# Linear attention with decay, then a GELU MLP, on one core: heads paired as h and h+4, reordered on chip, and an opening by single chunks

## Chip, core and metric

The kernel runs on one core of one Trainium2 chip. Its time is device time in microseconds (us). The core has a matmul engine (TensorE, "PE" in the profile, with its weight loads as "PEld"), a vector engine (VectorE, DVE), a scalar engine (ScalarE, ACT), GpSimd (POOL) and a queue engine (SyncE, SP). Matmul results go to PSUM, which has eight banks; 16 DMA engines move data, by transfers that POOL issues (loads that convert float32 to bf16) and SP issues (stores, and transposes of bf16 tiles within on-chip memory).

## The reference

Batch 4, 8 heads, sequence 768, head size 64; then an MLP with model width 512 and hidden width 2048, its rows being the 3072 tokens. Cut to what matters:

```python
def _attn_ref(q, k, v, lam):                      # q, k, v: (4, 8, 768, 64), lam: (8,)
    pos = np.arange(64); rel = pos[:, None] - pos[None, :]
    Dmask = np.where(rel >= 0, lam[:, None, None] ** rel[None], 0.0)
    lam_pow = lam[:, None, None] ** (pos[None, :, None] + 1)
    rev_pow = lam[:, None, None] ** (63 - pos[None, :, None])
    kv_state = zeros((B, H, D, D))
    for b in range(12):                           # blocks of 64 positions
        qb, kb, vb = ...
        intra = einsum('bhic,bhjc->bhij', qb, kb) * Dmask[None]
        intra = einsum('bhij,bhjd->bhid', intra, vb)
        inter = einsum('bhid,bhde->bhie', qb * lam_pow[None], kv_state)
        out[:, :, sl] = intra + inter
        kv_state = lam ** 64 * kv_state + einsum('bhsd,bhse->bhde', kb * rev_pow[None], vb)
    return out

h = x @ w_in                                      # x: (3072, 512), heads side by side
return 0.5 * h * (1 + erf(h / sqrt(2))) @ w_out   # exact GELU
```

## The kernel before

The sequence is cut into chunks of 128 positions: 6 per batch, 24 in all, chunk n being position block n // 4 of batch n % 4. Four chunks make a group (g = 0 to 5), which the MLP treats at once (512 tokens).

**Attention of a chunk.** q, k and v of all 8 heads are loaded by POOL as [128 positions, 8 heads, 64] (`load`, L66). k and q are transposed to [64 x 2 heads, 4 pairs, 128 positions]: a pair hp holds heads 2hp and 2hp+1, one in each half of the 128 partitions (HALVES). Chunks 0 to 7 are transposed by PE (`transposed`, L157) and copied out of PSUM by DVE or ACT; chunks 8 to 23 by a DMA that SP issues (`dma_transposes`, L173), straight from the loaded tile. Scores k q^T are 64-deep products per head (`scores` L179; from chunk 4 on in 64x64 quarters of the PE array, `scores_by_quarters` L190), masked by DVE (`masked` L199). Chunks from 4 on have a state per head (64x64), for two chunks in one tile: `from_states` (L222) multiplies it with qT, `from_values` (L231) adds masked scores times v. The output has the heads as the MLP's x wants them: head h in partition half h % 2 of column block h // 2. Since a state's half hi lies in row half hi and its output goes to column half hi, one product uses one of two diagonal quarters of the array; `turn` alternates the two chunks' banks, and eight dummy products (`apart`, L598 to 603) stand between the two turns where no scores do. The outputs leave PSUM by `empty_outputs` (L243) into xT, by ACT for chunks below 7, by DVE for chunk 7, and from chunk 8 on by DVE with the multiplication by lam_q (powers of lam along the position). For chunks 4 to 7 that multiplication is made in qT instead (`scaled`, L166). New states come from `next_products` (L203), `added` (L213) and `next_states` (L218). v times its decay, v_dec, is made by POOL (`decay_v`, L152).

**MLP.** First product and GELU in blocks (`mm1`, L421 and L424), second product for group 0 directly (`mm2`, L434), from group 1 on by seven half-size products instead of eight (`blocks_by_seven`, L277), for which DVE forms sums of GELU outputs (`g_sum`, L286) and of w_out (`w_out_sum`, L263).

**Order.** Each engine runs its own instructions in the order of the program. The opening (L495 to 541) is written out: attention of chunks 0, 1 and the transposes of 2, with dummy matmuls (`keep_warm`) in gaps; then the loop over MLP blocks (L672) puts attention work between blocks: group 0 by the table `group0` (L556; key i is ahead of block i, e = N1 is the first of the second product's 16 blocks), later groups by `todo`, a list of (place, function): place counts PE columns, B is one block of about 2048 columns, and "g + 10 * B" is ahead of block 10 of group g. A `visit` (L588) does the second half of attention for `done` chunks and scores for `asked` ones, on PE; `masks`, `empties`, `sums`, `new_states` are the DVE or ACT work behind it, placed separately. `begin_at` (L579) starts a chunk: DMA transposes on SP, v_dec on POOL. `prefetch` issues loads, 10 buffers for k and 8 each for q and v.

Group 0's plan of first-product blocks (kf is a column block of 128 of w_in):

```python
plan = [(kf, 1, two) for kf in range(6)] + [(0, 4, third), (4, 2, third)]
plan += [(kf, 1, three) for kf in range(6, 12)] + [(kf, 4, fourth) for kf in range(0, 12, 4)]
plan += [(kf, 1, slice(0, T)) for kf in range(12, NK2)]
```

Here `two` is chunks 0 and 1, `three` 0 to 2, `third` chunk 2, `fourth` chunk 3.

Of the kernel before, what the change touches and what calls it, by code (L numbers as in the profile page):

```python
# [15 lines left out]
def kernel(  # L16
# [14 lines left out]
    C = 128  # L31
# [82 lines left out]
    ln_col = consts.tile([128, HP], F32)  # L114
    lam_q = consts.tile([128, HP, C], F32)
# [9 lines left out]
    def make_powers():  # L125
        ln_r = ln.rearrange("p (hp hi) -> p hp hi", hi=2)
        for hi in range(2):
            p = slice(hi * D, (hi + 1) * D)
            nc.scalar.copy(ln_col[p, :, None], ln_r[p, :, hi:hi + 1])
        nc.scalar.activation(lam_m, ln, ACT.Exp, scale=negj)  # L130
        nc.scalar.activation(lam_c, ln_col, ACT.Exp, scale=float(C))
        for hp in range(HP):
            nc.scalar.activation(lam_q[:, hp, :], row, ACT.Exp, scale=ln_col[:, hp:hp + 1])
# [23 lines left out]
    def transposed(c, name, tag, empty):  # L157

        src, t_ps = getattr(c, name), bank([128, HP, C], BF16, tag, "t_ps")
        for hp in range(HP):  # L160
            nc.tensor.transpose(t_ps[:, hp, :], src[:, 2 * hp:2 * hp + 2, :], ident)
# [4 lines left out]
    def scaled(dst, src):  # L166
        nc.vector.tensor_mul(dst, src, lam_q)

    def transposes(c, tag="mh"):
        transposed(c, "k", tag, nc.scalar.copy)  # L170
        transposed(c, "q", "mh", scaled)

    def dma_transposes(c):  # L173
        c.kT = work_pool.tile([128, HP, C], BF16, tag="kT", name="kT", bufs=4)
        c.qT = work_pool.tile([128, HP, C], BF16, tag="qT", name="qT", bufs=6)
        nc.sync.dma_start_transpose(out=c.kT, in_=c.k.rearrange("p h d -> p (h d)"))
        nc.sync.dma_start_transpose(out=c.qT, in_=c.q.rearrange("p h d -> p (h d)"))
# [25 lines left out]
    def next_products(n, tag):  # L203

        kv_ps = bank([128, 2, HP, D], F32, tag, "kv_ps")
        for i, c in enumerate((live[n], live[n + 1])):
            for hp in range(HP):
                for hi, p in enumerate(HALVES):
                    nc.tensor.matmul(kv_ps[p, i, hp, :], c.k[:, 2 * hp + hi, :], c.v_dec[:, 2 * hp + hi, :],  # L209
# [12 lines left out]
    def from_states(chunks, o_ps, turn):  # L222

        for hp in range(HP):
            for hi, p in enumerate(HALVES):
                i = hi ^ turn
                c = chunks[i]
                nc.tensor.matmul(o_ps[i][p, hp, :], states[c.n - i][p, i, hp, :], c.qT[p, hp, :],  # L228
                                 start=(hp == 0), stop=False, skip_group_check=True)

    def from_values(c):  # L231
        v = c.v if c.early else c.v_dec
        for hp in range(HP):
            for hi, p in enumerate(HALVES):
                nc.tensor.matmul(c.o_ps[p, hp, :], v[:, 2 * hp + hi, :], c.sc_m[:, hp, hi, :],  # L235
# [478 lines left out]
```

## Time and profile before

| | us |
|---|---|
| median of 3 runs | 206.71 (205.24 to 207.11) |
| the profiled execution | 206.0 |
| its span | 204.2 |

| engine or line | busy us | instructions | mean ns |
|---|---|---|---|
| first product, 128x512 | 67.7 | 304 | 379 |
| GELU, ACT 128x512 | 52.6 | 88 | 597 |
| g_sum, DVE | 35.6 | 50 | 752 |
| masks without decay, DVE | 25.4 | 40 | 681 |
| v_dec, POOL | 24.8 | 23 | 1109 |
| x from o_ps with lam_q, DVE | 10.5 | 16 | 680 |
| state products, PE 64x64 | 8.0 | 160 | 219 |
| score products, PE 64x64 | 7.2 | 320 | 218 |
| x from o_ps, ACT | 4.0 | 7 | 586 |
| kT from t_ps, ACT | 2.4 | 4 | 588 |
| qT from t_ps, scaled, DVE | 2.8 | 4 | 688 |
| kT or qT from t_ps, plain, DVE | 3.4 | 8 | 421 |
| apart_ps, PE 64x64 | 1.5 | 32 | 216 |

A mean is the time of one instruction from start to end; PE's overlap, so that its slots are shorter. The profile's chain of waits, its last part in order of time, is followed back from the last instruction; it gives PE's slots.

### The profile page before, as it was taken

What the parts mean: (1) busy time and instruction counts of PE and PEld (TensorE: products, weight loads), DVE (VectorE), ACT (ScalarE), POOL (GpSimd) and SP (SyncE); (2) the same over time, 40 slices, a digit from 0 to 9 for tenths busy, and PEclk for the clock granted to TensorE, in tenths of its full rate; (3) what the DMA queues carried; (4) which work ended last, traced back from release to release, by engine and by line L of the source; (5) the groups of instructions that cost most, each with busy time, mean ns of one, the idle gap of its engine ahead of it and who ended that gap; (6) DMA issues with size and microseconds to landing.
All of it is one profiled execution on the core that took longest, in us unless ns stands there. A gap on an engine that the chain in (4) does not pass through costs nothing. (4 is left out here: it accounts for less than half of the span.)

```text
span 204.2 us, 4909 instructions
## 1 busy us (share of the span) xinstructions
PE 197.0 (96%) x2105; PEld 131.2 (64%) x2105; DVE 124.8 (61%) x202; ACT 80.7 (39%) x142; POOL 96.2 (47%) x112
## 2 busy tenths in 40 slices
PE   7889999999999999999999999999999999999992
PEld 2457574556874888646678646688645788445881
DVE  3743426773574699845999815968807857132482
ACT  4946653324565400273520273520264510477200
POOL 8999963899998922599998402000000000000000
PEclk9999999999999999999999999999999999999999
DMA  5999999999999999799999992200500000500014
GB/s 114 156 174 176 199 207 194 155 215 158 178 194 141 154 157 152 232 126 160 117 162 155 231 189 55 56 0 3 206 1 3 0 0 3 205 0 0 3 51 154
DMA packets 102373, 24.70 MB, mean 121 GB/s; under 512 B 92880, under 2 KB 99536, under 8 KB 102352
## 3 DMA queue, kind: packets, MB, share of 16 engines
q0 software_dynamic: 80688, 13.37, 89.4%
q1 hardware_dynamic: 21664, 11.02, 26.8%
q8 instruction: 16, 0.26, 0.5%
q14 instruction: 5, 0.04, 0.1%
HBM read 27.27 MB, written 6.29 MB: 164 GB/s over the span
## 5 line engine op out<-in xcount | busy, mean ns | idle before, releaser
L424 ACT ACTIVATE g_t<-h_ps 128x512 bf16<-128x512 f32 (+2 forms) x101 | 58.2, 576 | 82.0 <-PE h_ps L421 81.8
L421 PE MATMUL h_ps<-x_t,w_in_t 128*128 128x512 bf16 (+3 forms) x488 | 87.0, 334 | 0.4
L421 PEld LDWEIGHTS <-w_in_t 128*128 128x128 bf16 x488 | 44.1, 98 | 38.0 <-issue 1.3
L291 DVE TENSOR_TENSOR g_sum<-g_t 128x1024 bf16<-128x1024 bf16 x50 | 35.6, 752 | 12.6 <-ACT g_t L424 12.6
L317 PEld LDWEIGHTS <-g_sum 128*128 128x128 bf16 x400 | 38.6, 98 | 5.7 <-DVE g_sum L291 0.7
L155 POOL TENSOR_TENSOR v_dec<-v_t,lam_m 128x512 bf16<-128x512 bf16 x23 | 24.8, 1109 | 22.5 <-PE o_ps L235 10.2
L201 DVE TENSOR_TENSOR sc_m<-sc_ps,cmask 128x512 bf16<-128x512 f32 x40 | 25.4, 681 | 13.0 <-PE sc_ps L195 13.0
L68 POOL DMA_DIRECT2D k_t<-in_k_dram x24 | 22.3, 928 | 1.9 <-DMA w_out_t<-in_moe_w_out_dram 1.7
L68 POOL DMA_DIRECT2D v_t<-in_v_dram x24 | 21.7, 906 | 3.0 <-DMA w_out_t<-in_moe_w_out_dram 1.7
L68 POOL DMA_DIRECT2D q_t<-in_q_dram x24 | 21.8, 910 | 2.4 <-DMA w_out_t<-in_moe_w_out_dram 2.2
L317 PE MATMUL r_ps<-w_sum,g_sum 128*128 128x256 bf16 x160 | 19.1, 273 | 0.0
L317 PEld LDWEIGHTS <-g_t 128*128 128x128 bf16 x160 | 15.7, 98 | 2.9
L434 PE MATMUL o_ps<-w_out_t,g_t 128*128 128x512 bf16 x64 | 15.2, 379 | 0.0
L215 DVE TENSOR_TENSOR tmp<-kv_ps,state 128x512 f32<-128x512 f32 x8 | 5.1, 684 | 12.8 <-PE kv_ps L209 12.8
L251 DVE TENSOR_TENSOR x_t<-o_ps,lam_q 128x512 bf16<-128x512 f32 x16 | 10.5, 680 | 1.0 <-PE o_ps L235 1.0
L317 PE MATMUL p_ps<-w_out_t,g_sum 128*128 128x256 bf16 x80 | 9.7, 273 | 0.4 <-DVE g_sum L291 0.4
L434 PEld LDWEIGHTS <-g_t 128*128 128x128 bf16 x64 | 5.9, 98 | 6.2
L484 PE MATMUL idle_ps<-idle 128*128 128x256 bf16 (+1 forms) x33 | 8.6, 400 | 1.2 <-DVE idle L102 1.2
L317 PE MATMUL s_ps<-w_sum,g_sum 128*128 128x256 bf16 x80 | 9.6, 273 | 0.0
L317 PE MATMUL p_ps<-w_sum,g_t 128*128 128x256 bf16 x80 | 9.6, 273 | 0.0
L317 PE MATMUL q_ps<-w_sum,g_t 128*128 128x256 bf16 x80 | 9.6, 273 | 0.0
L317 PE MATMUL q_ps<-w_out_t,g_sum 128*128 128x256 bf16 x80 | 9.6, 273 | 0.0
(68 smaller groups left out, 153.4 us busy)
## 6 DMA issues: line engine op xcount, KB each, us to landing
out_dram<-o_sb SPq DMA_DIRECT2D x9, 512.0 KB, 2.8
k_t<-in_k_dram POOLq DMA_DIRECT2D x24, 128.0 KB, 6.9
q_t<-in_q_dram POOLq DMA_DIRECT2D x24, 128.0 KB, 7.4
v_t<-in_v_dram POOLq DMA_DIRECT2D x24, 128.0 KB, 7.3
w_out_t<-in_moe_w_out_dram POOLq DMA_DIRECT2D x4, 512.0 KB, 10.1
w_in_t<-in_moe_w_in_dram POOLq DMA_DIRECT2D x7, 256.0 KB, 7.3
out_dram<-o_sb SPq DMA_DIRECT2D x5, 256.0 KB, 6.0
wide_w<-in_moe_w_in_dram SPq DMA_DIRECT2D x1, 512.0 KB, 4.1
```

Of the source, the lines that this page charges most:

```text
L68: nc.gpsimd.dma_start(raw[n, name], chunk_of(name, n))
L155: eng.tensor_mul(c.v_dec, c.v, lam_m[:, :, None].to_broadcast((128, H, D)))
L201: nc.vector.tensor_mul(c.sc_m[:, :, hi, :], c.sc_ps[hi], mask)
L215: nc.vector.tensor_add(tmp, kv_ps, states[n])
L251: nc.vector.tensor_mul(c.x_o, c.o_ps, lam_q)
L291: nc.vector.tensor_tensor(gsum[i][:, ks, :], g_t[:, ka + k:ka + k + n4, ta], g_t[:, kb + k:kb + k + n4, tb], op=op)
L317: nc.tensor.matmul(o, left[i](k, slice(u * C, (u + 1) * C)), right[i](k), start=(begin and k == 0), stop=(k == KH - 1), skip_group_check=True)
L421: nc.tensor.matmul(h_ps[:, k, :], w_in_t[:, ki, (kf + k) * 128:(kf + k + 1) * 128], x_t[:, ki, cols], start=(k == 0 and ki == 0), stop=(ki ...
L424: nc.scalar.activation(g_t[:, kf:kf + ks, cols], h_ps, ACT.Gelu)
L434: nc.tensor.matmul(om[io], g_t[:, kf, io * C:(io + 1) * C], w_out_t[:, kf, :], start=(kf == 0), stop=(kf == NK2 - 1))
L484: nc.tensor.matmul(idle_ps[0][:, :cols], idle[:, :128], idle[:, :cols], start=True, stop=True)
```

## The change

Pairs are now heads h and h+4: partition half hi holds heads 4hi to 4hi+3. A state's row half is then the upper bit of the head, and its output's column half the lower bit, so that four state products in a row use four different quarters. To bring q and k into this order ahead of the transposes, a copy (`ordered`) makes k_p and q_p, two buffers each; chunks 0 to 3, which have no state to multiply, keep the old order. `apart` is gone. The scaling of chunks 4 to 7 by lam_q moves from qT to the emptying of o_ps (`emptied`), which is now by half of the heads for two chunks at once, and always on DVE.

```diff
     def make_powers():
         ln_r = ln.rearrange("p (hp hi) -> p hp hi", hi=2)
-        for hi in range(2):
-            p = slice(hi * D, (hi + 1) * D)
-            nc.scalar.copy(ln_col[p, :, None], ln_r[p, :, hi:hi + 1])
+        for hi, p in enumerate(HALVES):
+            nc.scalar.copy(ln_x[p, :, None], ln_r[p, :, hi:hi + 1])
+            nc.scalar.copy(ln_col[p], ln[p, hi * HP:(hi + 1) * HP])
...
     def transposes(c, tag="mh"):
         transposed(c, "k", tag, nc.scalar.copy)
-        transposed(c, "q", "mh", scaled)
-    def dma_transposes(c):
...
+        transposed(c, "q", "mh", nc.vector.tensor_copy)
+    def ordered(c, name, copy):
+        src = work_pool.tile([128, HP, 2, D], BF16, tag=name + "p", name=name + "_p", bufs=2)
+        copy(src, by_upper_bit(getattr(c, name)))
+        setattr(c, name + "_p", src)
+    def dma_transposed(c, name):
...
+        nc.sync.dma_start_transpose(out=dst, in_=src.rearrange("p s r d -> p (s r d)"))
...
-    def from_states(chunks, o_ps, turn):
-        for hp in range(HP):
-            for hi, p in enumerate(HALVES):
-                i = hi ^ turn
...
+    def from_states(chunks):
+        o_ps = [bank([128, 2, 2, C], F32, tag, "o_ps") for tag in ("o", "t")]
+        for i, c in enumerate(chunks):
+            for s in range(HP):
+                for hi, p in enumerate(HALVES):
+                    nc.tensor.matmul(o_ps[hi][HALVES[s % 2], s // 2, i, :], states[c.n - i][p, i, s, :], c.qT[p, s, :],
+                                     start=(i == 0 and s < 2), stop=False, skip_group_check=True)
...
+    def emptied(n, hi):
...
+        nc.vector.tensor_mul(xT[n // M][:, s, off:off + 2 * C].rearrange("p s (i t) -> p s i t", i=2), o_ps[hi],
+                             lam_q[:, s, None, :].to_broadcast((128, 2, 2, C)))
     def outputs(c):
...
+        empty = nc.vector.tensor_copy if c.n == 0 else nc.scalar.copy
...
-    N1 = 21
+    N1 = 19
...
+        plan = [(kf, 2, chunk) for chunk in (first, second) for kf in (0, 2)] + [(4, 2, two), (6, 2, two)]
+        plan += [(0, 4, third), (4, 4, third)]
+        plan += [(kf, 1, three) for kf in range(8, 12)] + [(kf, 4, fourth) for kf in range(0, 12, 4)]
...
+    nc.scalar.copy(w_in_t[:, :, :256], wide_w)
     make_powers()
...
-    nc.scalar.copy(w_in_t[:, :, :256], wide_w)
     keep_warm(2)
     scores(c)
-    keep_warm(9, new=False)
-    outputs(live[1])
-    c = early(2)
-    transposed(c, "k", "mh", copy)
-    transposed(c, "q", "mo", copy)
-    keep_warm(1)
+    early(2)
...
+        0: [lambda: keep_warm(2, new=False)],
+        1: [lambda: keep_warm(7), lambda: outputs(live[1])],
+        2: [lambda: k_transposed(2)],
+        3: [lambda: q_transposed(2)],
+        4: [lambda: scores(live[2]), lambda: keep_warm(7)],
+        5: [lambda: outputs(live[2])],
+        7: [lambda: k_transposed(3)],
+        8: [lambda: q_transposed(3), lambda: next_states(0, next_products(0, "t")), lambda: scores(live[3])],
+        10: [lambda: outputs(live[3])],
+        18: [lambda: next_states(2, next_products(2, "t"))],
+        e: [w_out_sums, lambda: both_ordered(4, copy), lambda: decay_v(live[4], nc.vector)],
         e + 8: [lambda: transposes(live[4])],
-        e + 9: [lambda: transposes(live[5], "o")],
+        e + 9: [lambda: both_ordered(5, nc.scalar.copy), lambda: transposes(live[5], "o")],
         e + 10: [lambda: visit([], [4, 5], "t o"), lambda: masks(5, 4)],
-        e + 11: [lambda: transposes(live[6])],
-        e + 13: [lambda: visit([4, 5], []), lambda: empties(4, 5)],
-        e + 14: [lambda: transposes(live[7])],
+        e + 11: [lambda: both_ordered(6, nc.scalar.copy), lambda: transposes(live[6])],
+        e + 13: [lambda: visit([4, 5], []), lambda: empties(4)],
+        e + 14: [lambda: both_ordered(7, nc.scalar.copy), lambda: transposes(live[7])],
...
+    def ordered_at(when, copy, *chunks):
+        for n in chunks:
+            for name in "kq":
+                at(when, lambda n=n, name=name: ordered(begun(n), name, copy))
+                at(when, lambda n=n, name=name: dma_transposed(live[n], name))
...
         if g == 1:
...
+            ordered_at(g - 0.07, nc.vector.tensor_copy, n)
+            ordered_at(g + 1 * B, nc.vector.tensor_copy, n + 1)
+            ordered_at(g + 6 * B, nc.vector.tensor_copy, n + 2)
+            ordered_at(g + 10 * B, nc.vector.tensor_copy, n + 3)
...
-            visit_at(g + 13 * B, [], [n, n + 1], (masks, n + 1, n))
+            visit_at(g + 14 * B, [], [n, n + 1], (masks, n + 1, n), banks="t o")
...
         for i, c_n in enumerate(later_on):
             begin_at(g + 0.57 + 0.03 * i, c_n)
+            if g == 1:
+                ordered_at(g + (19 + 2 * i) * B, nc.scalar.copy, c_n)
+            else:
+                ordered_at(g + (7 + i) * B, nc.vector.tensor_copy, c_n)
+            ordered_at(g + (27 + 2 * i) * B, nc.scalar.copy, c_n + 2)
```

`begin_at` now starts only v_dec; a chunk's copies and its DMA transposes have places of their own. In `visit`, the two calls of `from_states` with scores between them become one call ahead of everything else, and `from_values` takes both chunks at once.

More of the change, by code (lines that the diff above doesn't have):

```diff
@@ L254 @@
+        empty = nc.vector.tensor_copy if c.n == 0 else nc.scalar.copy
+        empty(xT[0][:, :, c.n * C:(c.n + 1) * C], o_ps)
     KH = NK2 // 2
@@ L298, in both @@
                 run()
[L299 to L305 removed]
+                if i in sums_at:
+                    g_sum((5, 2, 1, 6, 7)[sums_at.index(i)], 0)
+            return both
+        sums_at = range(10, 15)
+        blocks = [(with_sums(i, run), cost) for i, (run, cost) in enumerate(first)]
         left = {1: lambda k, t: gsum[1][:, k, t], 2: lambda k, t: gsum[2][:, k, t],
```

123 lines of the change are left out of this document (52 added, 71 removed).

## The prediction

> **What bounds the kernel now.** I read the page first: TensorE (PE) carries the span, and its granted clock never drops.
>
> ```profile
> span 204.2 us, 4909 instructions
> ...
> PE 197.0 (96%) x2105; PEld 131.2 (64%) x2105; DVE 124.8 (61%) x202; ACT 80.7 (39%) x142; POOL 96.2 (47%) x112
> ...
> PEclk9999999999999999999999999999999999999999
> ```
>
> The profiled execution took 206.0 us (1.8 around its span), 0.7 less than the median of the three timed runs, 206.7. The timeline of PE shows real work of the MLP beginning at 14.29 us and no gap worth naming afterwards but one of 0.41 us at 104.3 (p_ps waiting for DVE's g_sum). So a PE instruction that goes away after 14 us is worth its slot, unless something else then ends last. The chain of waits, read in order of time, prices the attention visits:
>
> ```profile
> 140.20 0.45 PE sc_ps L195 x28
> 140.65 0.22 PE o_ps L228 x8
> 140.87 0.57 PE o_ps L235 x16
> ...
> 169.34 0.34 PE o_ps L228 x8
> 169.68 0.22 PE apart_ps L602 x8
> 169.91 0.22 PE o_ps L228 x8
> 170.13 0.57 PE o_ps L235 x16
> ```
>
> Columns: start, length, what. Eight state matmuls (64x64 weights, 128 columns, two quarters of the array in turn) cost 0.22 us, 27 ns each; score matmuls of the same shape, which go round all four quarters, cost 0.45/28 = 16 ns each. Eight dummy apart_ps cost 0.22.
>
> The second limit shows in the first 55 us: the slices of the page have the DMA engines at 9 tenths there, and the timeline with each load's time to landing shows how close PE runs behind the data:
>
> ```profile
> 40.49 0.39 PE L161 MATMUL t_ps<-ident,k_t 128*128 128x128 bf16 x4
> ...
> 40.71 0.39 PE L161 MATMUL t_ps<-ident,q_t 128*128 128x128 bf16 x4
> ...
> 40.91 0.59 ACT L164 COPY kT<-t_ps 128x512 bf16<-128x512 bf16 x1 [0.46 <-PE t_ps L161]
> ```
>
> These are chunk 5's transposes. Its k was issued at 26.84 and landed 12.3 us later, at 39.1; its q at 28.36 and 11.6 later, at 40.0. PE has 0.7 us over q, no more.
>
> **The change, part by part.**
>
> *State matmuls.* Ten visits (two chunks each, 4 to 23) hold 16 of them, now 2 x 0.22. At the scores' rate they take 16 x 16 ns = 0.26; at an exact four at once, 0.22. Saving 0.18 to 0.22 per visit, 1.8 to 2.2 in all. *apart_ps:* four visits have it (32 instructions in the rows), 4 x 0.22 = 0.9 saved. Together 2.7 to 3.1; I take 2.9. The value matmuls keep number and shape.
>
> *Opening.* PE now does MLP blocks of chunk 0 alone while chunk 1's masks run, and of chunk 1 alone while chunk 2 loads. Chunk 0's x is ready when DVE has copied it, about 11.2 (outputs end at 10.4; DVE is at qT until 10.5, plus 0.69), if w_in's first 256 columns are cast by then: ACT does that right after the decay exponentials, 6.5 to 7.5; make_powers and the Gelu table move back by 1.05, the table is then in at about 10.8, before the first Gelu at 11.7. Following the landings (w_in 12.2, k2 13.1, q2 13.9, w_in 16.1 and 17.5), PE has finished the third chunk's block for kf 0 to 3 at 19.15 instead of 19.31, with eight columns of w_in (kf 0 to 7) done for chunks 0 and 1 instead of six; this surplus, two kf of 0.43 each, and the stalls of 0.2 to 0.3 that the new order fills bring the second half of group 0 (32.27 now) forward by 0.9 to 1.2. I take 1.05; k3, q3 (18.3, 20.0) and the last w_in (25.5) leave that room.
>
> *Where that goes.* Chunks 4 to 7 are now copied into the new order before PE transposes them. Chunk 4: DVE, behind the ten w_sum that end at 38.22 because they wait for w_out's landing; two copies, then PE, at 38.5 instead of 38.1. A DVE copy from SBUF to SBUF stands in no row: 0.42 (the copy from PSUM) above, about half of that below; I take 0.3. Chunk 5: ACT, two copies of 0.55 to 0.59 (the row of kT, same size), behind chunk 4's kT copy. q lands at 40.0, is copied by 40.6, PE transposes it at 40.65: 0.06 earlier than now. So of the 1.05 all but 0.06 is lost in front of chunk 5, and were there no gain in the opening, the ACT queue (39.86 + 3 x 0.48 + 0.11) would put q at 41.45, a loss of 0.75. Chunk 6 has 0.4 us over; chunk 7's q lands at 46.9, is ready at 47.5, and PE, 0.5 ahead by then, wants it at 47.55.
>
> *Emptying.* Chunks 4 to 7 no longer scale qT (4 x 0.27 of DVE saved), but ACT's three casts of x become scaled copies on DVE (0.68 each). x of chunks 6 and 7 is whole at about 54.8 and PE wants it at about 55.2: hidden, with 0.4 over.
>
> *Copies ahead of the DMA transposes, chunks 8 to 23.* Eight on DVE in group 1, eight more in groups 2 and 3 in a gap in which DVE idles 5.2 us, sixteen on ACT, which idles 12 us at the end of each group. By themselves they cost nothing; what matters is what they queue on. k_p and q_p have two buffers each, so chunk n+2's copy waits until chunk n's transpose has landed, 7 to 9 us after its issue at 53 to 60 us; and SP issues them one by one, 1.2 to 1.4 us each. Chunk 11: DVE's q copy waits for chunk 9's transpose (issued 54.1, landed about 62), is issued at 62.2 to 63.5, lands at 69.2 to 70.2; PE wants it at 70.4. DVE stands until 62.4 with five g_sums behind, which used to start at 58.5, but it has 5.1 us of idle time before 72. Zero, with 1.8 as the upper bound (landing 8.9 after 63.5).
> Chunk 17: its q copy sits on DVE in front of the `sums` of the visit at 92.8, and PE waits for these (they free the banks of its next products). q17 landed at 93.8, kv_ps was read at 94.33. Everything moves forward together, the load being released by PE's own kv_ps at 83.8, but the copy adds 0.3 and the later transposes of chunks 14 and 15 load the queue: 0 to 0.9, I take 0.2.
>
> Sum: 206.0 - 2.9 (visits) - 0.06 (opening less chunk 5's wait) + 0.2 (chunk 17) = 203.3; against the median of runs, 204.0. I give 203.6, between the two bases.
>
> **A rule that speaks against it.** Rows first: g_sum, 0.68 us as a rule, took 2.18 at 102.5 while POOL's v_dec ran (103.1 to 105.6), and two state products took 2.30 instead of 1.28 beside three v_dec. So DVE is held up by POOL on some operations, here with two SBUF operands; kT, qT and the masks, read from PSUM, are not. The Trainium skill (SBUF — State Buffer, "Who interferes with whom") makes it an exclusive lock, and puts a DVE copy from SBUF to SBUF in its fast two-port mode under it, against POOL's descriptor writing as well; no run here has such a copy yet. It is the third rival. For the price of such a copy, the Trainium skill (VectorE: DVE Perf Modes, "Mode 4×_2P — both tricks at once") would give an estimated 0.13 us of streaming for 512 bf16 elements, plus the fixed part; by it the sum would not change by 0.1.
>
> **The rivals.**
>
> 1. *The opening's gain survives* (chunk 5's q isn't what PE waits for, because loads land sooner or ACT copies faster than the rows say): up to 1.0 more, 202.3 to 203. Against it: landing times in that stretch are those of a full DMA queue, and the diff leaves the order of loads as it is. Chance 0.12.
>
> 2. *The two-buffer chain through DMA becomes the bound:* chunk 11 costs 1.8, chunk 17 0.9 instead of 0.2: 203.3 + 2.5 = 205.8 (206.2 as a median). For it: loads that land 8 to 11 us after their issue between 66 and 80 us; against it: loads of chunks 12 to 15 meet fewer transposes there than now. It decides from the point where a transpose takes over 7.5 us after 63. Chance 0.2.
>
> 3. *DVE's copies and POOL shut each other out.* POOL is busy nearly without break from 1.4 to 71 us. If each copy there stands behind a POOL instruction by the 1.5 us that g_sum did (2.18 - 0.68), then chunk 8's two copies push the masks of chunks 6 and 7 from 52.2 to about 54 with PE wanting them at 52.9 (1.0 lost), chunk 9's push x of chunks 6 and 7 past PE by 1.2, chunk 10's and 11's take DVE's reserve before the g_sums of m5, and chunk 17's costs 1.5: 3.7 at least, 206.8, slower than before (206.0); with rival 2's chunk 11, 208.6. It decides once the mean wait of a copy passes 1.2 us. Against it: POOL's rows of DMA issue show 0.88 to 0.95 whatever DVE does, so the hold may be a fraction of them. Chance 0.13.
>
> 4. *The quarters don't overlap:* state matmuls stay at 27 ns and only apart_ps goes: 206.0 - 0.9 - 0.06 + 0.2 = 205.2. Against it: scores show 16 ns with the same shapes, banks and order of quarters. Chance 0.05.
>
> **How the numbers follow.** My forecast, 203.6, has 0.5; its own range is 202.9 to 204.5 (the bounds of visits, of chunk 17, and the two bases). The range for 8 in 10 reaches to rival 1 below and rival 2 above: 202.2 to 206.3. About 1% is what a measurement of this kernel can tell (the three runs spread by 0.9%): under 204.6 is faster, over 208.8 slower. Faster: nearly all of the forecast (0.47), rival 1, and a few hundredths of 2: 0.62. Slower by more needs rival 3 with another one, and mishaps I haven't seen: 0.12. The rest, 0.26, lies between.
>
> **What would show it.** State matmuls: 16 in a row in about 0.26 us, visits without scores shorter by 0.4, with scores by 0.2; 32 instructions apart_ps gone. Opening: first products at 11 to 12 us instead of 14.3, the second half of group 0 at about 31.2. Chunk 5: PE idle by about 0.6 ahead of its q transposes, which stand at 40.6 to 40.8. Chunk 11: scores at 70 with no idle time. Chunk 17: PE idle at 92 to 93 by 0 to 0.9. If PE shows over 1 us idle between 45 and 110, or DVE's copies show over 1 us each, I'm wrong by rival 2 or 3; if state matmuls show 27 ns, by rival 4.

## The result, and the profile after

The changed kernel takes 210.96 us (median of 17 runs, 207.06 to 213.45) against 206.16 for the kernel before (17 runs beside them, 205.15 to 208.65). The ratio is 1.0107, with a 95% interval of 1.0065 to 1.0148: slower, by about 1% on that ratio and 2.3% on the medians. (The ratio is nearer to 1 because runs more than 1.5% above the fastest of their kernel are left out of it, which drops ten of the changed kernel's 17.) The profiled execution took 210.96 too, with a span of 209.2: 5.0 us above the 206.0 and 204.2 of before. Its mean granted clock is 0.984, and 14 of the 17 runs have one of 0.976 to 0.992; the three at 1.0 took 207.06, 207.53 and 208.40, so that the change costs 0.9 to 2.2 us even where the clock holds. Only the profiled run has a trace, and the account of the 5.0 us below is that run's.

The page of the changed kernel, its first lines:

```profile
span 209.2 us, 4990 instructions
...
PE 195.7 (94%) x2103; PEld 130.6 (62%) x2103; DVE 134.7 (64%) x224; ACT 90.7 (43%) x160; POOL 96.6 (46%) x112
...
PEclk9999999999999958999999999999999999999999
```

PE is busy for 1.3 us less than before, in a span that is 5.0 longer, and the granted clock, full everywhere before, drops in two slices, between 73 and 84 us. The waits of PE (what waited for what; us in total, how many, the longest) give the idle time a name:

```profile
PE sc_ps L202 <- DMA qT<-q_p: 3.8, 1, 3.8
PE h_ps L430 <- DVE tmp L223: 1.8, 1, 1.8
...
PE t_ps L163 <- ACT q_p L177: 0.5, 1, 0.5
...
PE t_ps L163 <- ACT k_p L177: 0.4, 1, 0.4
```

The first is chunk 11's scores, the second chunk 17's copy in front of `sums`, the last two chunk 5's transposes. The chain of waits of the changed kernel, in order of time (start, length, what), shows how the first came about:

```profile
56.72 7.85 DMA qT<-q_p
...
64.65 1.49 DVE q_p L177
...
66.16 8.91 DMA qT<-q_p
...
75.21 0.64 PE sc_ps L202 x14
75.85 1.00 PE o_ps L245 x16
76.84 3.49 PE p_ps L326 x16
80.33 1.75 PE q_ps L326 x16
...
115.98 0.35 PE o_ps L236 x16
116.33 0.45 PE sc_ps L202 x32
116.78 0.57 PE o_ps L245 x16
...
174.73 0.35 PE o_ps L236 x16
175.08 0.57 PE o_ps L245 x16
```

Chunk 9's q goes through the DMA (7.85 us) and frees its buffer; only then can chunk 11's q be copied into it (1.49), and only then go through the DMA itself (8.91). Behind the wait, sixteen matmuls of p_ps take 3.49 us and the next sixteen, of the same shape, 1.75. The last five lines answer to those shown of before: sixteen state matmuls take 0.35, where a visit without scores (169.34 to 170.13 in the chain of before) had 0.34, 0.22 of apart_ps and 0.22. A visit with scores now takes 1.36 instead of 1.58 us on the timeline (0.22 saved, six times), one without takes 0.91 instead of 1.36 (0.45, four times): 3.1 us in all. So the change does what it was made for, and loses more elsewhere.

Where, is read by setting the same instruction of the traces beside one another (start in us; the last two columns are experiments described below):

| place | before | after | e1 | e15 |
|---|---|---|---|---|
| group 0, second product | 32.27 | 31.92 | 31.93 | 32.03 |
| same, the block behind chunk 5's transposes | 40.93 | 41.80 | 41.75 | 41.73 |
| visit of chunks 6 and 7 | 52.52 | 52.96 | 52.90 | 52.88 |
| visit in front of chunk 11's scores | 70.81 | 70.80 | 70.75 | 70.73 |
| first p_ps behind that visit | 72.39 | 76.78 | 72.64 | 72.97 |
| next visit with scores | 92.83 | 98.21 | 92.53 | 92.86 |
| group 2, first p_ps | 100.25 | 107.09 | 101.39 | 100.18 |
| group 3, first p_ps | 130.96 | 136.78 | 131.09 | 131.05 |
| last group, first p_ps | 188.02 | 192.97 | 187.28 | 187.23 |
| last store's input (DVE) | 200.45 | 205.40 | 199.70 | 199.66 |

Up to 70.8 us the changed kernel is level: it gained 0.35 in the opening, lost 1.22 in front of chunk 5, gained 0.9 by two visits. At chunk 11 it loses 4.4 and, by the slow p_ps, 1.6 more; at chunk 17 another 1.76; from there to the end it wins back 1.9 (most of it by four more visits with scores, one without, and a wait of 0.41 for g_sum that before had and this one has not).

Why chunk 9's q went out so late is in the timeline of the changed kernel, DVE, POOL and SP's queue together (start, length, engine, line, operation):

```profile
49.22 1.06 POOL L156 TENSOR_TENSOR v_dec<-v_t,lam_m 128x512 bf16<-128x512 bf16 x1
49.40 1.04 DVE L177 COPY k_p<-k_t 128x512 bf16<-128x512 bf16 x1
...
50.21 0.92 POOL L68 DMA_DIRECT2D k_t<-in_k_dram  x1
...
50.36 0.28 DVE L177 COPY q_p<-q_t 128x512 bf16<-128x512 bf16 x1
...
52.87 0.89 POOL L68 DMA_DIRECT2D k_t<-in_k_dram  x1
52.96 0.92 DVE L177 COPY k_p<-k_t 128x512 bf16<-128x512 bf16 x1
...
53.73 0.90 POOL L68 DMA_DIRECT2D q_t<-in_q_dram  x1
53.80 1.12 DVE L177 COPY q_p<-q_t 128x512 bf16<-128x512 bf16 x1
54.41 2.20 SPq L184 DMA_TRANSPOSE kT<-k_p  x1
...
56.72 2.48 SPq L184 DMA_TRANSPOSE qT<-q_p  x1
...
63.98 0.92 POOL L68 DMA_DIRECT2D v_t<-in_v_dram  x1
...
64.65 1.48 DVE L177 COPY q_p<-q_t 128x512 bf16<-128x512 bf16 x1 [0.52 <-DMA qT<-q_p]
64.88 1.09 POOL L156 TENSOR_TENSOR v_dec<-v_t,lam_m 128x512 bf16<-128x512 bf16 x1
```

A copy by DVE takes 0.28 us at best, and 0.92 to 1.48 in four of these rows, which begin while POOL is in the middle of something: they end 0.12 to 0.29 after POOL's instruction does (49.22 + 1.06 = 50.28 against 50.44; 53.73 + 0.90 = 54.63 against 54.92). It makes no difference whether POOL multiplies (v_dec) or issues a load (52.87, 53.73). Not every copy beside POOL is held: the q copy at 50.36 follows another copy without a gap and is through in 0.28, though POOL had by then begun an issue (50.21). Nor do the two simply take turns: the copy at 64.65 stood through the rest of an issue (63.98 to 64.90) and the whole v_dec behind it. The Trainium skill (SBUF — State Buffer, "Who interferes with whom") says that a DVE copy in a two-port mode and GpSimd exclude each other from a shared port pair, the one that issues first holding it for its whole instruction, and counts descriptor writing in; the trace agrees with the holds, 0.92 behind an issue of a load and 1.04 behind a v_dec, while the 0.28 at 50.36 it leaves unexplained. ACT's copies of the same tiles are 0.62 or 0.63 in every row, with POOL busy or not.

The clock by stretches of the changed kernel (stretch, length, then busy time and count of PE, PEld, DVE, ACT, POOL; the granted clock is the third number from the end):

```profile
70.00:75.00 5.00, 1.44 (x40) 1.01 (x38) 4.05 (x5) 1.99 (x4) 3.12 (x4) 0.83 2.19 122
75.00:80.00 5.00, 4.79 (x48) 3.55 (x49) 4.11 (x7) 1.52 (x3) 1.86 (x2) 0.50 2.06 151
80.00:85.00 5.00, 5.00 (x69) 4.18 (x68) 4.73 (x9) 1.57 (x3) 0.00 (x0) 0.98 1.03 112
```

The clock falls to half at about 73.4, within the pause of 3.76, and is full again from 80.2, so that PE works for 5 us at half of it: that is p_ps's 3.49 instead of 1.75 and the value matmuls' 1.00 instead of 0.57, 2.2 us by rows together. Before had no pause above half a microsecond there, and no such row.

### The profile page after: what moved, and what is told of

Read it like the earlier page. It is cut to its first block, busy times and chain, and to the rows that moved or that the text cites. A ratio compares the mean times of both kernels' runs of the same rounds, so it can differ in the third digit from the quotient of the medians.

```text
span 209.2 us, 4990 instructions
## 1 busy us (share of the span) xinstructions
PE 195.7 (94%) x2103; PEld 130.6 (62%) x2103; DVE 134.7 (64%) x224; ACT 90.7 (43%) x160; POOL 96.6 (46%) x112
## 4 chain that ended last, share of the span: by engine, by line
PE 56%; DMA 23%; POOL 14%; DVE 4%; issue 1%; DVEq 0%; POOLq 0%
PE h_ps L430 23%; PE r_ps L326 8%; PE p_ps L326 8%; DMA qT<-q_p 8%; PE q_ps L326 8%; DMA v_t<-in_v_dram 5%; DMA q_t<-in_q_dram 5%; DMA w_out_t<-in_moe_w_out_dram 5%; PE s_ps L326 4%; POOL k_t L68 3%; POOL v_dec L156 3%; POOL v_t L68 3%; POOL w_in_t L89 2%; POOL q_t L68 2%; PE o_ps L245 2%
## 5 line engine op out<-in xcount | busy, mean ns | idle before, releaser
L430 PEld LDWEIGHTS <-w_in_t 128*128 128x128 bf16 x512 | 45.0, 98 | 38.3 <-issue 2.5
L326 PEld LDWEIGHTS <-g_sum 128*128 128x128 bf16 x400 | 39.5, 100 | 5.8 <-issue 0.2
L301 DVE TENSOR_TENSOR g_sum<-g_t 128x1024 bf16<-128x1024 bf16 x50 | 34.4, 730 | 11.1 <-ACT g_t L433 11.1
L252 DVE TENSOR_TENSOR x_t<-o_ps,lam_q 128x512 bf16<-128x512 f32 x20 | 13.1, 683 | 1.6 <-PE o_ps L245 1.6
L326 PE MATMUL p_ps<-w_out_t,g_sum 128*128 128x256 bf16 x80 | 11.2, 302 | 0.0
L202 PE MATMUL sc_ps<-qT,kT 64*64 64x128 bf16 x320 | 6.7, 222 | 3.8 <-DMA qT<-q_p 3.8
L177 DVE COPY k_p<-k_t 128x512 bf16<-128x512 bf16 x9 | 5.5, 607 | 6.8 <-DMA kT<-k_p 4.0
```

The source lines that it names most:

```text
L177: copy(src, by_upper_bit(getattr(c, name)))
L202: nc.tensor.matmul(c.sc_ps[hi][j, hp, :], c.kT[p, hp, j], c.qT[p, hp, :], start=True, stop=True, skip_group_check=True)
L252: nc.vector.tensor_mul(xT[n // M][:, s, off:off + 2 * C].rearrange("p s (i t) -> p s i t", i=2), o_ps[hi], lam_q[:, s, None, :].to_broadca ...
L301: nc.vector.tensor_tensor(gsum[i][:, ks, :], g_t[:, ka + k:ka + k + n4, ta], g_t[:, kb + k:kb + k + n4, tb], op=op)
L326: nc.tensor.matmul(o, left[i](k, slice(u * C, (u + 1) * C)), right[i](k), start=(begin and k == 0), stop=(k == KH - 1), skip_group_check=True)
L430: nc.tensor.matmul(h_ps[:, k, :], w_in_t[:, ki, (kf + k) * 128:(kf + k + 1) * 128], x_t[:, ki, cols], start=(k == 0 and ki == 0), stop=(ki ...
```

## The experiments

The theory after the result: chunk 11's q is late because two buffers tie it to chunk 9's transpose, because chunk 9's copies stand behind POOL, and because SP's queue passes the transposes one by one; the pause of PE then halves the clock. Chunk 17's copy on DVE costs 1.8 by itself. The rivals: the copies' durations alone do it, or the slow p_ps has another cause than the pause, or chunk 5 is the loss.

**e1: four buffers.**

```diff
-tag=name + "p", name=name + "_p", bufs=2
+tag=name + "p", name=name + "_p", bufs=4
```

> k_p and q_p with four buffers each instead of two; nothing else. Theory (the two-buffer chain): chunk 11's q copy no longer waits for chunk 9's transpose (landed 64.5), only for its own load (62.8); its transpose is issued at 63.5 to 64.5 instead of 66.2, lands at 71 to 73, and PE's idle time in front of chunk 11's scores falls from 3.8 us to 0 to 1.5, with no drop of the clock behind it: 3 to 5.5 us off the profiled 211.0, 205.5 to 208. Rival (the transposes' own time, 7 to 9 us from issue to landing with a queue full of loads, or SP's serial issue): the issue moves by under 1 us and the idle time stays above 3. Rival (DVE and POOL shutting each other out): the copies still take 0.6 to 1.5 us each and DVE reaches chunk 11 late whatever the buffers.

Measured: 206.91 (205.26 to 209.37), ratio 1.0013 (0.998 to 1.0047); profiled 205.26. On PE's timeline of this run the scores of chunk 11 (second line) wait 0.34 instead of 3.76, and p_ps is at its usual length:

```profile
71.00 0.39 PE L202 MATMUL sc_ps<-qT,kT 64*64 64x128 bf16 x16
71.72 0.42 PE L202 MATMUL sc_ps<-qT,kT 64*64 64x128 bf16 x16 [0.34 <-DMA qT<-q_p]
...
72.64 1.92 PE L326 MATMUL p_ps<-w_out_t,g_sum 128*128 128x256 bf16 x16
```

Chunk 11's q was issued at 63.82 (66.16 in the changed kernel) and landed at 71.6. The copies behind POOL are still there, and so is the wait of 1.8 at chunk 17. The buffers are what made the delay decisive. Four of the ten runs still have a mean clock of 0.984 to 0.992; they have no trace.

**e2: chunk 16's, 17's, 20's and 21's copies four blocks later**, behind the `sums` that PE waits for.

```diff
-ordered_at(g + (7 + i) * B, nc.vector.tensor_copy, c_n)
+ordered_at(g + (11 + i) * B, nc.vector.tensor_copy, c_n)
```

> The copies of chunks 16, 17, 20 and 21 move from blocks 7 and 8 to blocks 11 and 12 of groups 2 and 3, behind the sums of the visit at block 10. Theory: DVE's sums no longer stand behind chunk 17's q copy, which ended at 101.2 (load landed 99.8, copy 1.4); the 1.8 us that PE waited for tmp go away: 211.0 - 1.8 = 209.2. Rival: DVE is full behind the sums, and four copies there push the g_sums of m5 (0.7 to 1.4 us each beside POOL), so that PE waits as long a few us later: no change. The stall before chunk 11's scores stays as it is.

Measured: 209.09 (207.6 to 210.95), ratio 1.0147 (1.0076 to 1.0219). The waits of PE:

```profile
PE sc_ps L202 <- DMA qT<-q_p: 3.2, 1, 3.2
PE p_ps L326 <- DVE g_sum L301: 1.9, 1, 1.9
```

The wait for tmp is gone and one of 1.9 for g_sum has come in its place: the copies wait on DVE wherever they are put in that stretch, and whatever DVE has queued behind them is late. That the median met the theory's 209.2 is luck: the wait moved, as the rival had it, and the profiled run took 210.37, with a shorter wait at chunk 11 (3.2).

**e3: fourteen dummy matmuls (512 columns) between the scores of chunks 10 and 11**, added work, so that PE doesn't stand still.

```diff
         for n, tags in zip(asked, ("sc sc", banks)):
+            if banks == "mh mh" and n == asked[1]:
+                keep_warm(14, cols=512)
             scores_by_quarters(live[n], tags)
```

> 14 dummy matmuls of 512 columns (3.0 us) stand between the scores of chunk 10 and of chunk 11, where PE waited 3.8 us. They change no data. Theory (the clock drops because PE stood still): chunk 11's scores start when they did (75.2, set by the transpose), but the granted clock stays 1.00 and the first product of m5 takes 1.75 us instead of 3.49 and the value matmuls before it 0.57 instead of 1.00: 2.1 us faster than the changed kernel, 208.9. Rival (the clock drop has another cause, such as the four quarters at once): m5 stays at 3.5 us and the time at 211 or, where the stall would have been under 3.0 us, above it.

Measured: 211.44 (209.11 to 213.21), ratio 1.0248 (1.0184 to 1.0313); profiled 213.21. The clock by stretches of this run:

```profile
70.00:80.00 10.00, 10.00 (x129) 7.09 (x128) 9.07 (x13) 3.76 (x7) 4.82 (x5) 1.00 2.02 154
...
100.00:105.00 5.00, 3.25 (x8) 1.13 (x8) 5.00 (x8) 0.60 (x1) 4.38 (x5) 0.50 2.07 141
```

At chunk 11 the clock stays at 1.00 and p_ps takes 1.92 (3.56 on the changed kernel's timeline), at the same lateness of q: the pause was the cause. But the time did not fall by the two microseconds; of the four runs only one, 209.11, has a full mean clock and comes near the 208.9 of the theory. The profiled run had already waited 2.03 for k_t in the opening, with half the clock behind that, and its timeline shows a new pause at chunk 17:

```profile
98.23 2.86 DVE L177 COPY q_p<-q_t 128x512 bf16<-128x512 bf16 x1
98.80 2.14 POOL L156 TENSOR_TENSOR v_dec<-v_t,lam_m 128x512 bf16<-128x512 bf16 x2
...
101.75 3.57 PE L430 MATMUL h_ps<-x_t,w_in_t 128*128 128x512 bf16 x8 [3.86 <-DVE tmp L223]
```

The copy lasts over two v_dec, PE stands for 3.86, and the clock halves there. The same illness shows at the next place; that the repair brought it there is not shown.

How long a pause is too long can be read from all the traces, in slices of half a microsecond. No pause up to 1.9 (e2's second, e5) lowered the clock. Behind pauses of 2.03 (e3, opening), 2.46 (e6), 3.03 (e9) and 3.22 (e2) it was half for 3.4 us; behind 3.7 (e4), 3.76 (the changed kernel) and 3.86 (e3), for 6.8 us, begun within the pause. The Trainium skill (TensorE: Matmul & The Clock Gate, "What's actually happening") names half the clock after an idle window of about 3.4 us that runs freely; the two lengths agree with a window of that size, but four of these pauses are shorter than one, and there the measurement decides.

**e4: chunk 5's copies by DVE instead of ACT.**

```diff
-both_ordered(5, nc.scalar.copy)
+both_ordered(5, copy)
```

> Chunk 5's two copies are made by DVE (0.28 us each where POOL doesn't hold it) instead of ACT (0.62). Theory: PE's wait for chunk 5 (0.37 for k, 0.50 for q) is the load's landing (40.8) plus the copy: with DVE, q is ready at 41.1 instead of 41.5, k at 40.2 instead of 40.6, so 0.4 us less waiting at that place. At the end of the run this 0.4 is hidden, because the stall before chunk 11 is set by loads and transposes, not by PE: no change of the time beyond 0.2. Rival: PE is what counts all the way, and the run ends 0.4 us sooner.

Measured: 209.86 (206.48 to 211.15), ratio 1.011 (1.0028 to 1.0192). The wait at chunk 5 fell to 0.25, that at chunk 11 stayed (3.7), and so did the time. The run is a poor test of chunk 5: PE had waited 1.3 for w_in in the opening, the load of q was issued 1.1 later than in the changed kernel (29.44), and PE transposed q only at 42.12 (41.57). That what is won ahead of chunk 11 is lost there rests on the chain of the changed kernel, which up to chunk 11's q is made of POOL, DMA and DVE alone; it is argued and not shown.

**e5, e6: eight buffers of v_dec with four of k_p and q_p** (e6 with e4's edit too), to let POOL issue chunk 17's loads earlier.

```diff
-tag="vd", name="v_dec", bufs=7
+tag="vd", name="v_dec", bufs=8
```

> Four buffers for k_p and q_p, and eight instead of seven for v_dec. Theory: with four buffers what is left is PE's wait of 1.8 us for tmp at chunk 17, because DVE stands at chunk 17's q copy until that load has landed (93.7 to 94.5), and that load is held back on POOL by v_dec of chunk 15, which waits for PE's kv_ps (83.9) to free its buffer. With one buffer more POOL runs on at 78 to 79, loads 16 and 17 land by 90, and the 1.8 us go: 205.3 - 1.8 = 203.5 for the profiled run, and runs spread less. Rival: the earlier loads meet the transposes of chunks 12 to 15 and the stores, so that those land later and a new wait takes the place of the old one: 205. Rival: the copy's own time beside POOL (1.0 to 2.9 us at chunk 17) is what counts, not the landing: under 0.7 us gained.

> As before it, and chunk 5's copies by DVE instead of ACT. Theory: once no later wait hides it, the 0.6 to 0.9 us that PE waits for chunk 5 count, and DVE's copy (0.28 against 0.62) gives back 0.4 to 0.6: 203.0. Rival: PE then comes earlier to chunk 7's or chunk 11's transposes, which are set by landings, and waits there: no gain.

Measured: e5 206.26 (204.24 to 209.51), ratio 0.9993 (0.9963 to 1.0023); e6 207.29 (204.59 to 209.58), ratio 1.0016 (0.9981 to 1.0051). Both missed. In e5 the loads were not issued earlier; in e6 they were, at 81.4, and chunk 17's q landed at 97.0 all the same, among the transposes, with a wait of 2.5 for tmp and half the clock behind it (24 matmuls of h_ps in 6.92 instead of 5.34).

**e7: four buffers and the opening of before** (the opening's part of the diff undone).

> The changed kernel with four buffers, but with the opening of the kernel before (plan of group 0, places of chunks 0 to 3, w_in's cast behind the powers, chunk 0 emptied by ACT). To be read against the four-buffer kernel (profiled 205.3). Theory: the opening brings at most 0.1, since chunk 5 waits for a landing whatever the opening does: 205.2 to 205.8, q of chunk 5 transposed within 0.3 us of 41.5. Rival (the opening's gain survives): 0.4 to 1.0 slower than the four-buffer kernel, 205.7 to 206.3, with chunk 5 that much later.

Measured: 205.59 (204.71 to 208.98), ratio 0.9975 (0.995 to 0.9999), against e1's 206.91 with the new opening. The second product starts at 32.23 (31.93 in e1), and chunk 5's q is transposed at 41.50 (41.52 in e1): the 0.3 us are gone nine microseconds later. The single-chunk blocks are worth nothing here. The medians lie further apart than that because four of e1's ten runs have a lowered mean clock, and one of e7's twelve.

**e8: the kernel before with eight buffers of v_dec**, a control: e5's one edit without the change.

> A control: the kernel before with eight instead of seven buffers for v_dec. Theory: there DVE does not stand at a load, so the earlier loads of chunks 16 and 17 change nothing but up to 0.4 us (the wait for g_sum at 104): 0.0 to 0.4 us faster. Rival: v_dec's buffer is worth as much to the old kernel as to the new, 1 us or more, and then the gain of the run before this one has nothing to do with the copies.

Measured: 205.38 (205.16 to 205.94), ratio 0.997 (0.9947 to 0.9993). The wait of 0.41 for g_sum is gone.

**e9, e10, e11: no copies for chunks 4 to 7.** PE transposes them head by head from the loaded tile (half-wide transposes), with four buffers (the first part of the diff below is in all three, the second in e10 and e11); e9 with the opening of before, e10 the same with chunk 17's and 21's copies on ACT at block 12, e11 as e10 with the new opening.

```diff
-            nc.tensor.transpose(t_ps[:, hp, :], src, ident)
+            if c.early:
+                nc.tensor.transpose(t_ps[:, hp, :], src, ident)
+            else:
+                for hi, p in enumerate(HALVES):
+                    nc.tensor.transpose(t_ps[p, hp, :], getattr(c, name)[:, hi * HP + hp, :], ident)
...
-                ordered_at(g + (7 + i) * B, nc.vector.tensor_copy, c_n)
+                ordered_at(g + (7 + 5 * i) * B, nc.scalar.copy if i else nc.vector.tensor_copy, c_n)
```

> Four buffers, the old opening, and no copies for chunks 4 to 7: PE transposes each head by itself into its half of the partitions (16 transposes of 64 columns of weights per chunk instead of 8 of 128). Theory: the copies of chunks 5 and 7 stand between a landing and PE; without them PE doesn't wait for chunk 5 (0.4 in the run with the old opening), at the same PE time if two half-wide transposes run side by side: 0.3 to 0.5 at that place. At the end of the run most of it is lost again at chunk 11 or 17, which are set by landings: 0 to 0.4 us. Rival: half-wide transposes take a full slot each: 4 x 8 x 55 ns = 1.8 us slower by chunk 7.

> The one before, and chunk 17's (and 21's) copies moved from DVE at block 8 to ACT at block 12, between GELUs. Theory: DVE's sums no longer stand behind chunk 17's load, so that PE's wait of 1.7 to 1.9 us for tmp goes and with it the drop of the clock in the runs where it was longer than 3 us; ACT takes two copies of 0.62 into GELU gaps of 0.27 and PE has two banks in reserve: 1.2 to 1.8 us faster than the kernel with the old opening, about 204.0 (profiled), runs closer together, faster than the kernel before by 0.7 to 1.0 percent. Rival (a new wait, as when the copies stood behind the sums on DVE): ACT's copies or the later transpose of chunk 17 make PE wait at GELU's banks or at chunk 17's scores: no gain.

> The same with the new opening. Theory: what kept the opening's gain (0.35 at the start of the second product) from lasting was chunk 5's copy behind its load; without the copy PE waits for the landing alone (40.0 to 40.8), and 0.0 to 0.35 of it last to chunk 8: equal to the one before within 0.4 us. Rival: the new opening is dearer by itself (chunk 3's transposes and x wait behind DVE), 0.4 us or more slower than with the old one, as the two four-buffer kernels suggest (medians 206.9 and 205.6).

Measured: e9 206.52 (204.78 to 211.26), ratio 1.0002 (0.997 to 1.0034), with a wait of 3.0 for tmp; e10 205.38 (204.68 to 206.48), ratio 0.9984 (0.9959 to 1.001); e11 206.26 (204.88 to 208.27), ratio 1.0001 (0.9961 to 1.0041). In e10 the wait for tmp is gone; instead PE waits 1.0 for g_t, behind ACT's copies, and 0.8 for g_sum. e11 answers the question of the opening, on PE's timeline:

```profile
40.74 0.41 PE L166 MATMUL t_ps<-ident,k_t 128*64 128x128 bf16 x8 [0.27 <-DMA k_t<-in_k_dram]
41.62 0.41 PE L166 MATMUL t_ps<-ident,q_t 128*64 128x128 bf16 x8 [0.47 <-DMA q_t<-in_q_dram]
```

With no copy in between, and the second product begun at 31.86, PE waits for the load itself. The landing of chunk 5's q is a wall; whoever comes to it earlier waits there. It is not a fixed one: q landed at 40.0 before, at 40.8 in the changed kernel, at 40.6 in e10 and at 41.6 in e11. By the medians e11 is 0.9 slower than e10, by the profiled runs 1.0 faster, and e14 and e15 below are level, so whether the new opening costs something by itself stays open.

**e12: four buffers, the opening of before, chunk 5's copies by DVE, chunk 17's and 21's by ACT** (k at block 11, q at block 14).

```diff
+                if i == 0:
+                    ordered_at(g + 7 * B, nc.vector.tensor_copy, c_n)
+                else:
+                    for name, w in (("k", 11), ("q", 14)):
+                        at(g + w * B, lambda n=c_n, name=name: ordered(begun(n), name, nc.scalar.copy))
+                        at(g + w * B, lambda n=c_n, name=name: dma_transposed(live[n], name))
```

> Four buffers, the old opening, chunk 5's copies on DVE, and chunk 17's (and 21's) on ACT apart from each other: k at block 11, q at block 14, so that ACT works off the first before the second comes. Theory: what kept the 3.1 us of the visits in the last runs were (a) 0.2 per chunk for half-wide transposes, gone here, (b) 0.5 in groups 2 and 3 each, when two copies in a row held GELU up, gone here: 0.8 to 1.8 us less than the run with half-wide transposes and ACT (profiled 204.3), so 202.7 to 203.5, and runs as close together; faster than the kernel before by 0.5 to 1.3 percent. Rival (the loads set the pace up to block 10 of group 2, whatever PE saves): PE waits at chunk 11's scores and at g_sum instead, 204 to 204.5, no difference from the kernel before.

Measured: six runs in two bunches, 203.59, 204.40, 204.94 and 207.02, 207.03, 207.13, all with a granted clock near 1.0. The ratio is 0.9898 (0.983 to 0.9966), but it rests on the lower three, and the median of all six, 205.98, is that of before beside it, 205.87. No claim is made on it; what parts the bunches stays open.

**e13: the changed kernel, two buffers as it has, with chunks 8's and 9's copies by ACT.**

```diff
-            ordered_at(g - 0.07, nc.vector.tensor_copy, n)
-            ordered_at(g + 1 * B, nc.vector.tensor_copy, n + 1)
+            ordered_at(g - 0.07, nc.scalar.copy, n)
+            ordered_at(g + 1 * B, nc.scalar.copy, n + 1)
```

> The changed kernel with its two buffers; only the copies of chunks 8 and 9 are made by ACT (0.62 each) instead of DVE, where they took 0.3 to 1.1 us each. Theory (DVE's copies wait for POOL's instruction, and the two-buffer chain passes the delay on): chunk 9's q transpose is issued at 54 to 55 instead of 56.7, lands at 62 to 63 instead of 64.5, chunk 11's q transpose is issued at 63.5 to 64.5 instead of 66.2, and PE's idle time in front of chunk 11's scores falls from 3.8 us to 1.3 to 2.3, mostly without a drop of the clock: 1.5 to 4 us off the time. Rival (the buffers and the transposes' 8 us alone make the chain; POOL's hold is too small to matter): idle time within 0.7 of 3.8 and the time unchanged. Rival: ACT's copies of chunk 9 hold GELU up behind the load (landed 52.2) and PE waits there instead.

Measured: 208.15 over four runs (205.18, 206.96, 209.34, 214.83), ratio 1.0104 (1.0011 to 1.0197); the profiled one is the fastest, with a span of 203.4. Its timeline:

```profile
63.54 0.62 DVE L177 COPY q_p<-q_t 128x512 bf16<-128x512 bf16 x1 [0.43 <-DMA qT<-q_p]
...
64.46 1.30 SPq L184 DMA_TRANSPOSE qT<-q_p  x1
...
71.01 0.95 PE L202 MATMUL sc_ps<-qT,kT 64*64 64x128 bf16 x32
```

Chunk 9's q is issued 0.8 earlier (55.94), chunk 11's q 1.7 earlier, and it lands at 71.5: the scores of both chunks run as one group, 0.95 long instead of 0.62, so that some 0.3 of waiting is left. So the hold by POOL was needed for the stall too; without it two buffers are just enough in this run. They have nothing in hand, and the other runs, up to 9.7 us longer, two of them with a mean clock of 0.988 and 0.976, fit runs in which the transpose came later again; these have no trace, so that is argued and not shown.

**e14, e15: all the known waits taken away together.** e14 is e12 with e13's edit; e15 is the changed kernel with four buffers, e13's edit and e12's for chunk 17.

> Four buffers for k_p and q_p, the opening of before, chunk 5 copied by DVE, chunk 17 copied by ACT (k at 11 blocks, q at 14), and in addition chunks 8 and 9 copied by ACT instead of DVE. Theory (the visits' saving of 3.1 us is there, and what eats it is the waits behind the copies): PE's waits at chunk 11 (0.8 in the run without this edit) go to 0, ACT's two extra pairs (2.5 us) delay g_t at most once by 0.3, and the time is 0.5 to 0.8 below that run: median 205.2, best near 203.0, ratio 0.987 to 0.992. Rival (the saving is given back somewhere that no wait on a copy shows): the waits go and the time stays at 206, ratio 0.995 to 1.0.

> The changed kernel with its own opening, four buffers for k_p and q_p, chunks 8 and 9 copied by ACT, chunk 17 copied by ACT (k at 11 blocks, q at 14). Chunk 5 stays on ACT. Theory: like the run beside it, but PE stands 0.9 in front of chunk 5 for ACT's copies, and is 0.3 to 0.4 earlier from the opening: 0.3 to 0.5 slower than that run, 205.6. Rival (the opening costs nothing in front of chunk 5): same time as the run beside it.

Measured: e14 205.45 (204.38 to 206.38), ratio 0.9979 (0.9954 to 1.0005); e15 205.27 (204.26 to 206.9), ratio 0.9984 (0.9957 to 1.001), beside 205.58 for before. By their numbers the rival holds; its reason holds in part. In e14 the wait at chunk 11, which was to go to 0, is 0.7, though chunk 9's copies no longer stand behind POOL, and 0.9 are lost on DVE's f_x, which is no copy. The waits of PE in e15:

```profile
PE sc_ps L202 <- DMA qT<-q_p: 0.7, 1, 0.7
PE q_ps L326 <- DVE g_sum L301: 0.6, 1, 0.6
...
PE t_ps L163 <- ACT k_p L177: 0.4, 1, 0.4
PE t_ps L163 <- ACT q_p L177: 0.3, 1, 0.3
```

The waits on copies and transposes did not go, they shrank. In the table above e15 is 0.80 late behind chunk 5, loses 0.7 at chunk 11 and 0.6 at g_sum, 2.1 together; of the 3.1 that the visits save, and the 0.41 that before waits for g_sum, 1.4 should be left, and the last line stands 0.79 ahead of before. The saving is there, and the reordering eats most of it, 2.1 us in small waits that the view lists and 0.6 in places that it doesn't; what is left is less than the measurement can tell.

No version with the change in it beats the kernel before by more than a fraction of a per cent on all its runs; e8, the kernel before with one buffer more (0.997), is as good as the best of them and has none of the copies.

## Why the prediction was wrong

**The visits: right.** 2.7 to 3.1 was forecast and 2.9 taken; the timeline shows 3.1. Sixteen state matmuls run at the scores' rate (70.80 to 71.05 on PE's timeline, 0.25 for 16), and apart_ps is gone. Rival 4 is out. The emptying was hidden, as forecast: no wait of PE for x stands in the view.

**The opening: a size off.** 1.05 was forecast, 0.35 measured. It changed nothing in the sum, since, as the prediction had it, chunk 5's landing takes back whatever comes to it early (e7, e11).

**Chunk 5: right in kind, short in size.** "Chunk 5's wait" of 1.0 less the opening's gain was to leave 0.06 gained; it left 0.87 lost. PE waits 0.37 for k and 0.50 for q, whose transposes stand at 41.57, not at 40.6 to 40.8: the load landed at 40.8 in this run instead of 40.0, and ACT's queue put k's copy at 39.99. (The figure for the case without a gain, 39.86 + 3 x 0.48 + 0.11, is 41.41 and not 41.45.) It was not what decided the time: at 70.8 us the kernel is level again, and the chain to chunk 11's q doesn't pass through PE.

**Chunk 11: the step that failed.** The prediction wrote "Zero, with 1.8 as the upper bound". Measured: 3.76 of waiting. It had drawn the chain rightly (chunk 9's transpose, chunk 11's copy, chunk 11's transpose), and named the three lengths wrongly: chunk 9's q was issued at 56.7, not 54.1, since its copies took 0.92 and 1.12 instead of 0.3 and SP's transposes 2.2 and 2.5 in the queue instead of 1.2 to 1.4 (the trace of before has one of 2.71 at 59.40); chunk 11's copy took 1.49 instead of 0.3; so the last issue came at 66.16, not by 63.5, and the landing took 8.91. Even by its own figures the bound is 2.0 (63.5 + 8.9 = 72.4 against 70.4). An upper bound made of one late member is no bound for a chain of five in which each can be late. e1 and e13 each take one member away, and the stall falls to some 0.3 in both.

**The clock: a term that was missing.** 2.2 us, the second largest loss, stands nowhere in the prediction, which read a full clock in before and carried it over. The pause that the change makes is what takes it away (e3). Nothing in the trace of before could have shown it, since its longest wait of PE after 14 us is 0.41.

**Chunk 17: mis-sized.** 0 to 0.9, with 0.2 taken; 1.76 measured. The q copy stood behind POOL (1.43), on a load that landed at 99.8.

**The rivals.** 2 and 3 came together, at the places that were named for them. The prediction priced that pair at 208.6 without the clock. Against rival 3 it had set that "POOL's rows of DMA issue show 0.88 to 0.95 whatever DVE does"; those rows belong to the engine that holds, and say nothing of the one that waits. Nor was the point of decision right, "once the mean wait of a copy passes 1.2 us": the mean k_p copy on DVE took 0.61, a wait of 0.33, and the two or three copies that lie on the chain decided it.

**The sum, mended.** As written it comes to 203.24, given as 203.3. With what was measured: 206.0 − 3.1 (visits) − 0.35 (opening) + 1.22 (chunk 5) + 3.76 (chunk 11) + 2.2 (clock) + 1.76 (chunk 17) − 0.41 (the g_sum wait of before, gone) = 211.1, against 210.96.

## What to carry to other kernels

A saving on the busiest engine is only worth what the new feeding path lets through: where a change puts a copy in front of a transfer, write out the whole chain from buffer to buffer (release, copy, queue, transfer, release) with each member at its slowest row, and give it buffers until it has a member's length in hand. A pause of PE of 2 us or more was paid twice in these traces, by the pause and by the clock behind it, so in a kernel that runs at full clock a forecast of 1.8 us of waiting and one of 3.8 are not on one line. What a small DVE copy costs is read from what POOL does at that moment, including its issuing of loads.

## What was not expected of the hardware

- A DVE copy of 128x512 bf16 within on-chip memory: 0.28 us at best, up to 1.48 in the changed kernel when begun during an instruction of POOL, 2.86 across two v_dec (e3). Issuing a load holds it as multiplying does.
- The granted clock stayed full behind pauses of PE up to 1.9 us and halved behind every one from 2.03 up, for 3.4 us or for 6.8. One such stretch of 3.4 us at half takes 0.008 off the mean clock of a run of 207 us, so the mean that each run lists tells roughly how many it had: 0.992 in e6 and e9, which had one, 0.984 in the profiled run of the changed kernel, which had the length of two, 0.976 in e3, which had three.
- A DMA transpose of 128x512 bf16 lands 2.4 us after its issue at 127 us, where the queues are nearly empty, and 7 to 9 us between 54 and 75, where loads and transposes share the queues: a factor that no single row of it shows.
- Half-wide transposes on PE (64 columns of weights, two for each pair) brought chunk 5's q forward with the opening of before (41.02 in e10, 41.50 in e7 with the copy) and not with the new one (41.62 in e11), but added gaps of some 0.2 us in front of the next matmuls: taking out the copy was not free either.
